# Output stores of two chunks on ScalarE's queue, and the first chunk's skip term added by VectorE: a change to a tuned state-space and feed-forward kernel

## The chip, the core and the metric

The kernel runs on one core of a Trainium2 chip. The metric is the device time of one execution in microseconds (us); several executions of each kernel were taken, and medians are quoted. An execution counts as fast or slow by its time and by the clock that TensorE was granted; ratios use the fast ones alone. The engines are TensorE (PE in the profile; PEld is its weight load), VectorE (DVE), ScalarE (ACT), GpSimd (POOL) and SyncE (SP), each with its own stream of instructions.

## The reference, cut to what matters

```
xn  = layernorm(x)                                    # x: 2048 tokens x 448, bf16
Bu  = xn @ B_bar.T                                    # complex
h_t = Lam_bar * h_{t-1} + Bu_t                        # recurrence over the tokens
s   = 2 * Re(h @ C.T) + xn * Dskip                    # the last product is the "skip"
g   = silu((silu(xn @ w_gate) * (xn @ w_up)) @ w_down)
out = x + s * g
```

The kernel takes the tokens in four chunks of 512, each of four blocks of 128 tokens.

## The kernel before: the parts that the change and the argument touch

The names in the profile: `gp`, `up` are the gate and up products, `gs`, `us` their values in SBUF, `Vt` their product, `hd` the down product, `sg` its silu; `pb` is the product with B, `ere`, `eim`, `bu_re`, `bu_im`, `H_re`, `H_im`, `tmp` belong to the recurrence; `y` is the product of the state with C; `t`, `ob` are the output's temporaries; `xT` is the normed input turned by DMA transposes that SyncE issues.

One chunk's output, and its skip term. In the kernel before, the first chunk's skip (and that of the last block) is made by TensorE with a diagonal matrix `Dd`; for the others VectorE multiplies and adds it:

```python
SKIPS = [(q, j) for q in (1, 2, 3) for j in range(TQ)][:-1]     # where VectorE adds the skip

def finish(q, j, y, sg, eng=nc.sync, c0=0, c1=D):
    ...
    if (q, j) in SKIPS:
        nc.vector.tensor_tensor(out=t[:], in0=y, in1=skip[q][:, j, c0:c1], op=ALU.add)
        y = t[:]
    nc.vector.tensor_tensor(out=t[:], in0=y, in1=sg[:, c0:c1], op=ALU.mult)
    ob = work.tile([P, c1 - c0], BF16, name="ob", **of)          # two buffers
    nc.vector.tensor_tensor(out=ob[:], in0=t[:], in1=x_all[:, m, c0:c1], op=ALU.add)
    eng.dma_start(out=out2d[m * P : (m + 1) * P, c0:c1], in_=ob[:])
```

The products that split K, the dimension that a matmul sums over, into two halves (`pb`, `gp`, `up`) run in two passes, and the second pass may start only after the first has finished. This notice travels by a no-op in GpSimd's stream:

```python
def tell(mm):
    told = nc.gpsimd.nop(nofuse=True)                            # waits for the matmul mm
    tc.add_manual_dep(told.ins, mm.ins.name, SYNC, reason="share")
    return told.ins.name

def sums(q, pairs, between=None):
    left = []
    for share, first in ((0, True), (1, False)):
        for n, two in enumerate(pairs):
            ...                                                  # the matmuls
                    if not first and m == 0:
                        told_of(mm, left[n])                     # second pass waits for the no-op
            if first:
                left.append(tell(mm))
```

The norms of the third and fourth chunk: ScalarE sums and squares (`junk`), GpSimd makes the root (three small operations), ScalarE then norms:

```python
def act_root(q):                                                 # on GpSimd
    nc.gpsimd.tensor_scalar(out=vep[...], in0=sums_of[:, 1, :], ...)
    nc.gpsimd.tensor_tensor(out=rstd[...], in0=vep[...], in1=halves[:], op=ALU.pow)
    nc.gpsimd.tensor_tensor(out=off_of[:, 1, :], in0=off_of[:, 0, :], in1=rstd[...], op=ALU.mult)
```

The order of the middle of the program:

```python
turned_norms(8, 9, 10, 11)           # ScalarE norms of the third chunk, SyncE's transposes
outs(0, sg)                          # output of the first chunk
sg = downs(1, 2.4, {
    0: act_sums((12, 13, 14), 0) + [on(skips, 2)],
    1: act_sums((15,), 0) + [act_means] + act_sums((12, 13), 1),
    2: act_sums((14, 15), 1) + [on(act_root, 3)],                # roots of the fourth chunk
})
drive(2, 4.8)                        # pb of the third chunk
gu(2, bg, 2.4)                       # gate and up of the third chunk
```

## Time and profile before

| | |
|---|---|
| time | 187.42 us (median of 4, 186.88 to 187.54) |
| span of the profiled execution | 185.0 us |
| busy: TensorE, VectorE, ScalarE, GpSimd | 177.9, 160.1, 120.2, 13.4 us |
| TensorE's one gap in the middle | 1.26 us, before `hd` of the third chunk |
| VectorE's one long gap | 7.7 us, before the first chunk's third `ob` |

What it does not show, and what decided the case, is GpSimd. Its timeline in the kernel before (columns: start, length, engine, line, operation, and in brackets the idle time and what ended it), in the middle of the program:

```profile
88.44 0.39 POOL L274 TENSOR_SCALAR vep<-sums_of 128x4 f32<-128x4 f32 x1 [11.50 <-ACT junk L263]
88.92 1.01 POOL L278 TENSOR_TENSOR rstd<-vep,halves 128x4 f32<-128x4 f32 x1
90.00 0.22 POOL L281 TENSOR_TENSOR off_of<-off_of,rstd 128x4 f32<-128x4 f32 x1
```

These are the fourth chunk's roots: GpSimd waits for ScalarE's last square, then works until 90.22. The second of them, the power operation, ends at 88.92 + 1.01 = 89.93. TensorE's timeline of the same time:

```profile
89.04 5.47 PE L455 MATMUL pb<-xT,BT 64*128 64x512 bf16 x56
```

The 56 `pb` matmuls of the third chunk run in one piece. The first passes of the first two products (16 matmuls) take 1.73 us at the pace of 0.216 us a pair, so TensorE needs the notice at 89.04 + 1.73 = 90.77. When could it have had it? In the five profiles below in which TensorE waits for these roots (the changed kernel, e5 to e8), it goes on 0.11 or 0.12 us after the power operation has ended; the third root operation, which still runs then, does not hold the notice. That makes 89.93 + 0.11 = 90.04 here. The reserve was thus about 0.7 us (an estimate from these times), and no row of the page shows it.

### The profile page before, as it was taken

Reading aid. Unit: us, or ns where it says so; the run is one execution under the profiler, and the core shown is the slowest. Engines: PE = TensorE matmul, PEld = TensorE weight load, DVE = VectorE, ACT = ScalarE, POOL = GpSimd, SP = SyncE. Lnnn points to the kernel's source line nnn. Section 1 sums busy time; section 2 is a strip of 40 time slices with the busy share of each in tenths; the row PEclk is TensorE's granted clock in tenths of the full one; section 3 lists DMA queues with packets and bytes.
Section 4 is the critical chain, followed back from the end, with each engine's and each line's share of the span. In section 5 each row is a group of like instructions: output and inputs, shape, how many; then the busy total and the mean of one; then the engine's idle time right before and its main releaser. Section 6 shows DMA issues by size and latency. Waiting matters only on the chain.

```text
span 185.0 us, 3723 instructions
## 1 busy us (share of the span) xinstructions
PE 177.9 (96%) x1449; PEld 87.8 (47%) x1449; DVE 160.1 (87%) x254; ACT 120.2 (65%) x247; POOL 13.4 (7%) x25
## 2 busy tenths in 40 slices
PE   7899999999999999999999999979999999999991
PEld 3574444544444555555454444535454444455551
DVE  4649799999999999902999999999999999999583
ACT  3247879997789999498499556962259696512110
POOL 7332200000000000600300000000000000000000
PEclk9999999999999999999999999999999999999999
DMA  5899655979200000043100000042100000001111
GB/s 160 209 277 338 124 94 112 132 167 377 101 0 0 5 0 0 0 86 81 50 2 4 2 0 4 0 82 70 62 4 0 0 4 0 0 4 50 50 50 50
DMA packets 26129, 12.71 MB, mean 69 GB/s; under 512 B 16000, under 2 KB 26112, under 8 KB 26112
## 3 DMA queue, kind: packets, MB, share of 16 engines
q1 hardware_dynamic: 24896, 12.06, 25.3%
q10 hardware_dynamic: 1088, 0.41, 0.8%
q8 instruction: 11, 0.18, 0.4%
q14 instruction: 6, 0.05, 0.1%
q0 software_dynamic: 128, 0.00, 0.0%
HBM read 7.23 MB, written 1.84 MB: 49 GB/s over the span
## 4 chain that ended last, share of the span: by engine, by line
PE 67%; DVE 25%; DMA 3%; issue 2%; ACT 1%; POOL 0%; SPq 0%; DVEq 0%
PE gp L455 20%; PE hd L597 16%; PE up L455 15%; PE pb L455 9%; PE y L626 7%; DVE bu_re L527 5%; DVE bu_im L527 4%; DVE tmp L521 2%; DVE Vt L589 2%; DVE ob L648 2%; DMA out_dram<-ob 2%; DVE t L645 2%; DVE H_im L521 2%; DVE ere L521 1%; DMA x_all<-in_A_x_dram 1%
## 5 line engine op out<-in xcount | busy, mean ns | idle before, releaser
L455 PE MATMUL gp<-xT,Wg 64*128 64x512 bf16 (+1 forms) x413 | 85.8, 365 | 0.4 <-ACT xT L304 0.3
L455 PE MATMUL up<-xT,Wu 64*128 64x512 bf16 (+1 forms) x413 | 85.8, 365 | 0.0
L455 PEld LDWEIGHTS <-Wg 64*128 64x128 bf16 x413 | 38.5, 94 | 25.1 <-issue 0.4
L455 PEld LDWEIGHTS <-Wu 64*128 64x128 bf16 x413 | 38.4, 94 | 19.7 <-POOLq L437 0.5
L581 ACT ACTIVATE gs<-gp 128x512 bf16<-128x512 f32 x56 | 33.7, 604 | 19.6 <-PE gp L455 11.7
L597 PE MATMUL hd<-Wd,Vt 128*128 128x448 bf16 x224 | 43.4, 353 | 1.3 <-DVE Vt L589 1.3
L585 ACT ACTIVATE us<-up 128x512 bf16<-128x512 f32 x54 | 32.9, 609 | 0.0
L597 PEld LDWEIGHTS <-Vt 128*128 128x128 bf16 x224 | 21.8, 98 | 22.0 <-DVE Vt L589 1.7
L602 ACT ACTIVATE sg<-hd 128x448 bf16<-128x448 f32 x16 | 8.6, 538 | 25.2 <-PE hd L597 20.6
L455 PE MATMUL pb<-xT,BT 64*128 64x512 bf16 (+1 forms) x224 | 21.9, 349 | 0.0
L648 DVE TENSOR_TENSOR ob<-t,x_all 128x448 bf16<-128x448 f32 (+2 forms) x17 | 10.2, 597 | 8.2 <-DMA out_dram<-ob 7.7
L589 DVE TENSOR_TENSOR Vt<-gs,us 128x2048 bf16<-128x2048 bf16 (+1 forms) x16 | 17.2, 1079 | 0.0
L455 PEld LDWEIGHTS <-BT 64*128 64x128 bf16 x224 | 10.7, 94 | 11.4 <-issue 0.7
L626 PE MATMUL y<-C,H_re 128*128 128x448 bf16 (+2 forms) x68 | 15.7, 342 | 0.0
L527 DVE TENSOR_TENSOR_SCAN bu_re<-rcol,H_re,ere 128x512 bf16<-128x512 f32 x12 | 14.9, 1262 | 0.1
L488 ACT ACTIVATE bu_re<-pb 128x512 bf16<-128x512 f32 (+1 forms) x20 | 10.1, 537 | 2.7 <-PE pb L455 2.6
L626 PE MATMUL y<-C,H_im 128*128 128x448 bf16 (+2 forms) x51 | 11.9, 342 | 0.0
L498 ACT ACTIVATE bu_im<-bu_re 64x512 bf16<-64x512 bf16 x16 | 10.0, 628 | 2.1 <-DVE bu_re L527 1.8
L527 DVE TENSOR_TENSOR_SCAN bu_im<-rcol,H_im,eim 128x512 bf16<-128x512 f32 x9 | 11.4, 1262 | 0.0
L287 ACT ACTIVATE xn<-x_all,off_of,rstd 128x384 bf16<-128x384 bf16 (+1 forms) x16 | 8.1, 588 | 2.8 <-POOL off_of L281 2.8
L521 DVE TENSOR_TENSOR tmp<-bu_im,ST 128x2048 bf16<-128x2048 bf16 x8 | 9.7, 1218 | 0.0
L626 PEld LDWEIGHTS <-H_re 128*128 128x128 bf16 x68 | 6.4, 98 | 6.1 <-issue 0.4
(98 smaller groups left out, 174.5 us busy)
## 6 DMA issues: line engine op xcount, KB each, us to landing
out_dram<-ob SPq DMA_DIRECT2D x15, 112.0 KB, 1.7
Wd<-in_B_w_down_dram SPq DMA_DIRECT2D x1, 1568.0 KB, 9.0
x_all<-in_A_x_dram SPq DMA_DIRECT2D x1, 896.0 KB, 5.5
Wg<-in_B_w_gate_dram SPq DMA_DIRECT2D x2, 384.0 KB, 7.0
Wu<-in_B_w_up_dram SPq DMA_DIRECT2D x2, 384.0 KB, 7.6
x_all<-in_A_x_dram SPq DMA_DIRECT2D x1, 448.0 KB, 5.7
Wg<-in_B_w_gate_dram SPq DMA_DIRECT2D x1, 288.0 KB, 3.1
Wu<-in_B_w_up_dram SPq DMA_DIRECT2D x1, 288.0 KB, 4.2
```

What stands on the lines that cost most here:

```text
L455: mm = nc.tensor.matmul(out, lhsT=w[h, d, :], rhs=xT[h, d, q * W + c0 : q * W + c1], start=(first and m == 0), stop=(not first and m == 3 ...
L488: nc.scalar.activation(to, pair[i][0], ACT.Copy)
L498: nc.scalar.activation(out[a], in_[b], ACT.Copy)
L521: nc.vector.tensor_tensor(out=of(out, n), in0=of(a, n), in1=of(b, n), op=op)
L527: nc.vector.tensor_tensor_scan(out=T["b"][c][:, k, :], data0=rcol[:, k : k + 1].to_broadcast([P, W]), data1=T["e"][c][:, k, :], initial=in ...
L581: nc.scalar.activation(gs[:, i + j, :], gp_[:], ACT.Silu)
L585: nc.scalar.activation(us[:, i + j, :], up_[:], ACT.Copy)
L589: nc.vector.tensor_tensor(out=Vt[:, f0 : f0 + n, :], in0=gs[:, 0:n, :], in1=us[:, 0:n, :], op=ALU.mult)
L597: nc.tensor.matmul(hd, lhsT=Vt_of[q][:, fi, j * P : (j + 1) * P], rhs=Wd[:, fi, :], start=(fi == 0), stop=(fi == NF - 1),)
L602: nc.scalar.activation(sg[:], hd, ACT.Silu)
L626: nc.tensor.matmul(y[:, c0:c1], lhsT=h, rhs=C2[:, n, c0:c1], start=(n == 0), stop=(n == NS - 1))
L648: nc.vector.tensor_tensor(out=ob[:], in0=t[:], in1=x_all[:, m, c0:c1], op=ALU.add)
```

## The change

Its intent: stores that sit on SyncE behind the transposes hold VectorE for 7.7 us, so ScalarE issues the stores of the first two chunks; and TensorE is the bound, so the first chunk's skip matmuls go to VectorE. The first chunk's norms have been overwritten by then, so ScalarE makes them again, into the tile that takes the skip. The smaller number in `downs` is the VectorE work that is slipped in between the blocks; with it, steps of the recurrence move behind the output. Cut to its core:

```diff
-    SKIPS = [(q, j) for q in (1, 2, 3) for j in range(TQ)][:-1]
+    SKIPS = [(q, j) for q in range(NQ) for j in range(TQ)][:-1]
...
+    def first_norms():
+        for j in range(TQ):
+            nc.scalar.activation(
+                skip[0][:, j, :], x_all[:, j, :], ACT.Identity, bias=off_0[:, j : j + 1],
+                scale=rstd[:, j : j + 1],
+            )
...
-    def outs(q, sg, hooks={}):
+    def outs(q, sg, eng=nc.sync):
         for j in range(len(sg)):
-            finish(q, j, out_sum(q, j), sg[j])
+            finish(q, j, out_sum(q, j), sg[j], eng)
...
-    sg = downs(0, 1.8, {
+    sg = downs(0, 1.3, {
...
-        2: act_sums((10, 11), 1) + [on(act_root, 2), on(skips, 1)],
+        2: act_sums((10, 11), 1) + [on(act_root, 2), on(skip_tile, 0), on(skip_tile, 1),
+                                    first_norms, on(skips, 1)],
+        3: [on(skips, 0)],
     })
...
-    outs(0, sg)
+    outs(0, sg, nc.scalar)
...
-    outs(1, sg)
+    outs(1, sg, nc.scalar)
```

More of the change, by code (lines that the diff above doesn't have):

```diff
@@ L258 @@
     off_of = ctile([P, 2, TQ], F32, "off_of")
+    off_0 = ctile([P, TQ], F32, "off_0")
     def act_sum(n, squares):
@@ L605, with skip_tile @@
     skip = {}
-    SKIPS = [(q, j) for q in (1, 2, 3) for j in range(TQ)][:-1]
+    SKIPS = [(q, j) for q in range(NQ) for j in range(TQ)][:-1]
+    def skip_tile(q):
+        skip[q] = work.tile([P, TQ, D], BF16, name="skip", tag="nz")
     def skips(q):
-        skip[q] = work.tile([P, TQ, D], BF16, name="skip", tag="nz")
         for j in range(TQ):
-            for c0, c1, x0 in ((0, KF * P, 0), (KF * P, D, KF * P + R)):
+            parts = [(0, KF * P, 0), (KF * P, D, KF * P + R)] if q else [(0, D, 0)]
+            for c0, c1, x0 in parts:
+                normed = xn[j][:, x0 : x0 + c1 - c0] if q else skip[q][:, j, :]
                 nc.vector.tensor_tensor(
-                    out=skip[q][:, j, c0:c1], in0=xn[j][:, x0 : x0 + c1 - c0],
-                    in1=skip["row"][:, c0:c1], op=ALU.mult,
-                )
+                    out=skip[q][:, j, c0:c1], in0=normed, in1=skip["row"][:, c0:c1], op=ALU.mult
+                )
+    def first_norms():
[4 more added lines that the diff above has]
+            )
     def out_sum(q, j, k0=0, k1=KT):
@@ L721, in drive @@
             params_out()
+            nc.vector.scalar_tensor_tensor(
+                out=off_0[:], in0=mv[:, 0:TQ, 0], scalar=-1.0, in1=rstd[:, 0:TQ],
+                op0=ALU.mult, op1=ALU.mult,
+            )
         ssm_steps(bg, q)
@@ L732, in downs @@
         return sg
-    def outs(q, sg, hooks={}):
+    def outs(q, sg, eng=nc.sync):
         for j in range(len(sg)):
-            finish(q, j, out_sum(q, j), sg[j])
-            for fn in hooks.get(j, ()):
-                fn()
-    def do(fns):
-        for fn in fns:
-            fn()
+            finish(q, j, out_sum(q, j), sg[j], eng)
     gu(0, bg, 0.0, {
@@ L772 @@
     turned_norms(8, 9, 10, 11)
-    outs(0, sg)
+    outs(0, sg, nc.scalar)
     sg = downs(1, 2.4, {
-        0: act_sums((12, 13, 14), 0) + [on(skips, 2)],
+        0: act_sums((12, 13, 14), 0) + [on(skip_tile, 2), on(skips, 2)],
         1: act_sums((15,), 0) + [act_means] + act_sums((12, 13), 1),
@@ L782 @@
     turned_norms(12, 13, 14, 15)
-    outs(1, sg)
-    sg = downs(2, 2.4, {1: [on(skips, 3)]})
+    outs(1, sg, nc.scalar)
+    sg = downs(2, 2.4, {1: [on(skip_tile, 3), on(skips, 3)]})
     drive(3, 4.8)
```

## The prediction

> **What bounds the kernel now.** I read the page's busy row first, then the chain of waits, the list of who waited for whom, and the timeline of each engine from 57 us on.
>
> The page, part 1, and two groups of its part 5:
>
> ```profile
> PE 177.9 (96%) x1449; PEld 87.8 (47%) x1449; DVE 160.1 (87%) x254; ACT 120.2 (65%) x247; POOL 13.4 (7%) x25
> ...
> L597 PE MATMUL hd<-Wd,Vt 128*128 128x448 bf16 x224 | 43.4, 353 | 1.3 <-DVE Vt L589 1.3
> ...
> L648 DVE TENSOR_TENSOR ob<-t,x_all 128x448 bf16<-128x448 f32 (+2 forms) x17 | 10.2, 597 | 8.2 <-DMA out_dram<-ob 7.7
> ```
>
> TensorE is busy for 177.9 of 185.0 us. Its starts show it streaming at a steady pace (a pair of K=64 matmuls every 0.216 us, a 448-column one every 0.19 us), so this is real work. In the timeline its only gap between about 19 and 181 us is one of 1.26 us, before `hd` of the third chunk, where it waits for the last `Vt` of that chunk. VectorE's one long gap is 7.7 us, for a store to land. The chain of waits ties the two together:
>
> ```profile
> 81.74 0.61 ACT junk L263 x3
> 82.36 0.31 issue
> 82.86 0.36 SPq L309
> 83.32 3.33 DMA out_dram<-ob
> 86.74 0.64 DVE ob L648
> ...
> 120.64 1.12 DVE Vt L589
> 121.75 1.21 DVE bu_im L527
> 122.98 0.96 DVE H_im L521
> 123.94 0.61 DVE Vt L589
> 124.60 8.50 PE hd L597 x44
> ```
>
> (Start, length, work.) The stores of the first chunk sit on SyncE behind four transposes whose inputs ScalarE makes from 76.98 to 81.02 us. The first store is issued at 83.32 and lands at 86.65. `ob` has two buffers, so the third `ob` waits. VectorE then works without a gap until 123.94+0.61, where TensorE has lost 1.26 us. From 124.6 us TensorE streams again until about 181; after that comes the tail of the last chunk, which the change leaves alone. So 7.7 us of VectorE waiting cost only 1.26 us of time.
>
> **What the Trainium skill says.** "PSUM — Partial Sum Buffer", Engine vs sequencer instructions: "ScalarE/VectorE/GpSimdE queues are strict FIFO." That decides this case: a store put into ScalarE's stream waits there for its `ob`, and all of ScalarE's later work waits with it. The trace shows the like on SyncE (stores behind transposes). "DMA: Bandwidth & Descriptors", Issuing engines are not separate DMA queues: transfers of different issuers run on the same 16 DMA engines and interleave, and only issue time is saved. So a store issued by ScalarE among the transposes need not land faster; here stores took 1.7 us in the median, and 3.3 us right behind the transposes. "VectorE: DVE Perf Modes", The perf-mode tier table: tensor_tensor runs at 2x on bf16 in SBUF and at 1x with an fp32 or PSUM operand. The trace agrees: 0.62 us for 128x448 with `y` from PSUM, against 0.35 us for the 128x384 bf16 `skip`.
>
> **The change part by part.**
>
> 1. TensorE: 16 skip matmuls of the first chunk go. Its four `y` start at 72.27, 73.79, 75.31 and 76.83, 1.52 us apart; those of the second chunk, without skip matmuls, start 1.33 us apart (115.59, 116.93). Saved: 4 x 0.19 = 0.75 us, on TensorE's path. All other TensorE work keeps its order.
>
> 2. VectorE: four skip products of 128x448 (an estimate from 0.37 us for a 384+64 pair: about 0.3 each, 1.2 in all), four additions at 0.66 us of spacing (2.6), and one tiny operation (0.2, like its neighbours at 36 to 38 us). Added: 4.0 us.
>
> 3. ScalarE: four norms of 128x448 at about 0.6 us (as the squares and the `c_tb` of this size) = 2.4 us. They come after the last squares (73.68 us) and before `sg` of the fourth block, in the hole of 2.77 us in which ScalarE waits for GpSimd's roots (73.68+0.53 to 76.98). So they are nearly free to ScalarE: 73.68+2.4+0.5 = 76.6, and the next norms still begin at 76.98 and end at 81.02.
>
> 4. Order: the smaller budget puts two steps (`tmp`, `ere`: 1.14+1.24) of the second chunk's recurrence behind its output instead of before it, and a scan and an `H_im` step (1.2+0.9 = 2.1 us) of the third chunk behind its last `Vt`. The comparison of the instruction orders shows this.
>
> VectorE in the new order: `H_re` done at 65.1 (+0.2); four `C` paced by `c_tb`, to 68.4; `eim`, to 69.2; eight skip products, 70.7; `tmp` and `eim`, 72.6. Then it must wait for the new norms, made at 74.3 to 76.1. That is a new wait of about 2.8 us in all: skip products done at 76.5, `ere` at 77.7. Four outputs at 2.05 us (the pace of 124.46, 126.50, 128.55): `ob` at 79.7, 81.8, then the third. ScalarE can issue the first store only after its norms, at 81.05, and it lands between 82.8 and 84.4 (1.7 to 3.3 us); the third `ob` would start at 83.1, so it waits 0 to 1.3 us. Outputs done at 86 to 87.2. Third chunk's skips 1.5, `tmp` and `ere` 2.4: the scans start at 89.9 to 91.1, where they started at 90.2. Of the 7.7 us, then, 4 go to new work, 2.8 to a new wait, and up to 1.3 stay: nearly nothing is left. The last `Vt` of the third chunk profits by the order alone: 2.1 us earlier, so at about 122.2 to 123.4 instead of 124.55.
>
> ScalarE: the fourth store is issued at 86.4 to 87.6; call it S. Only then can it turn to `sg` of the second chunk's first block, done before at 81.2. From there to the last of these `sg` it needs the work of 81.2 to 88.36 without its gaps, plus one `sg`: about 7.0 us. So the last `sg` ends at S+7.0 = 93.4 to 94.6, and before at 89.7.
>
> TensorE: `hd` of the second chunk would end 0.75 us earlier, at 88.4; the first `pb` group takes until 91.1 (2.65), and 0.86 later its second group turns to the packed pair, which takes the PSUM banks of the last two `hd` (eight banks in rotation: four `hd`, four `pb`, then these). They are free only after that last `sg`. So TensorE stops at 92.0 and goes on at 93.5 to 94.7: a new wait of 1.5 to 2.7 us. The gate and up matmuls of the third chunk then start at 95.0 to 96.2 instead of 94.35, that is 0.65 to 1.85 later. The 1.26 us lost before `hd` goes in exchange, since `Vt` is now there first. Net for the rest of the program: -0.6 to +0.6 us. TensorE's path in one sum: -0.75 (skip matmuls) -1.26 (wait for `Vt`) +2.1 (wait for the bank, the middle) = +0.1.
>
> The second set of stores on ScalarE costs nothing: before, `sg` of the third chunk waited for VectorE anyway (2.40 us for `t`, at 125.83), since `sg` has four buffers. By the same steps its fourth store comes near 131.5 and the last `sg` near 134.5, before the packed `pb` pair at about 136. VectorE's total up to the last chunk is unchanged within 1 us, and it had 1.9 us to spare there (its wait for `y` at 174.36).
>
> **The rivals.**
>
> A, the intended one: ScalarE gets through in time, and both small gains come to TensorE: 0.75+1.26 = 2.0 us, so 185.4 us. For it: TensorE has no other gap, and the packed `pb` pair was reached about 3 us after its `sg` in the trace (92.7 against 89.7). Against it: the fourth store holds ScalarE some 5 us longer than that.
>
> B, the one that I take: a wait for a PSUM bank behind ScalarE replaces the wait for `Vt`. The sum gives 187.5; if the stores land quickly and ScalarE's work packs tighter, 186.6.
>
> C, VectorE stays the bound: if the first store lands late and the new norms are slower, the scans start over 1.5 us later, the `Vt` come later in the third and fourth chunk, and ScalarE is held longer: 188 to 188.5. For it: VectorE has next to no reserve from 86 to 172 us, and gets 4.0 us more work. Against it: 2.1 us have moved behind the critical `Vt`.
>
> **Range and chances.** The three ways lie between 185.4 and 188.5. I give B the greatest weight and move the point a little towards A, since S rests on the landing of one store and on estimates for the norms, both taken on the slow side: 187.0 us, 185.7 to 188.1 eight times in ten. A gain over 2% (3.7 us) would need more than TensorE's gap and the removed matmuls together, and nothing else before 181 us is idle: 1 in 50. A loss over 2% would need a stall of ScalarE that holds up TensorE for over 5.7 us: 1 in 50. Within 2%: 0.96.
>
> **What would show it.** The steps are right if the profile of the changed kernel has: no wait of 7.7 us before `ob`, but one before the `skip` products for ScalarE's norms, near 73 us; ScalarE without work for about 5 us after 81 us and `sg` of the second chunk not before 86 us; a gap of TensorE before `pb`, released by ScalarE's `sg`, near 92 us; and no gap before `hd` near 124 us. The prediction is wrong if TensorE has no gap at `pb` (then A), if it still waits for `Vt` near 124 us (then C), or if stores and norms on ScalarE open a gap in the gate and up matmuls, which I put at none.

## More of the kernel before

One row of part 5 of the page does show that TensorE waits on GpSimd's sequencer at all (POOLq, at the line of the no-op), earlier in the program:

```profile
L455 PEld LDWEIGHTS <-Wu 64*128 64x128 bf16 x413 | 38.4, 94 | 19.7 <-POOLq L437 0.5
```

## The result, and the profile after

The changed kernel took 193.19 us (median of 4, 192.67 to 193.74), the kernel before 187.42. The ratio is 1.031 (95% interval 1.028 to 1.035): slower. Ratios here are the mean time of one kernel's fast runs over that of the other's in the same rounds, so not quite the ratio of the medians. The predicted 187.0 is 6.2 us too low, and the upper end of its range (185.7 to 188.1) 5.1 us.

The page of the changed kernel, parts 1, 2 and 5 (the clock row is the granted TensorE clock in tenths, in 40 slices of the span):

```profile
PE 179.2 (94%) x1433; PEld 87.8 (46%) x1433; DVE 164.3 (86%) x263; ACT 122.5 (64%) x251; POOL 13.0 (7%) x25
...
PEclk9999999999999999999969999999999999999999
...
L598 PE MATMUL hd<-Wd,Vt 128*128 128x448 bf16 x224 | 43.2, 352 | 0.0
...
L456 PE MATMUL pb<-xT,BT 64*128 64x512 bf16 (+1 forms) x224 | 23.6, 366 | 5.5 <-POOLq L438 5.5
...
L660 DVE TENSOR_TENSOR ob<-t,x_all 128x448 bf16<-128x448 f32 (+2 forms) x17 | 10.2, 598 | 1.1 <-DMA out_dram<-ob 0.6
```

Both waits that the change aimed at are gone: `hd` waits 0.0 us, and `ob` 0.6 us for a store where it was 7.7. In their place, `pb` waits 5.5 us for the line of the no-op in GpSimd's sequencer. And one slice has a clock of 0.6. The chain of waits shows how it came to that (start, length, work; the short pieces named "issue" are left out):

```profile
85.43 0.64 DVE ob L660
86.08 0.34 ACTq L661
86.47 0.54 ACT sg L603
87.01 1.67 ACT junk L264 x6
88.68 0.43 ACT sg L603
89.11 0.56 ACT junk L264 x2
89.70 0.21 ACT off_of L271
89.94 1.41 ACT junk L264 x4
91.35 0.43 ACT sg L603
91.78 1.31 ACT junk L264 x4
93.17 0.43 POOL vep L275
93.67 1.91 POOL rstd L279
95.62 0.03 POOLq L438
95.69 5.29 PE pb L456 x40
100.99 0.21 PE gp L456
```

Read it from the top. VectorE ends the fourth `ob`; ScalarE issues its store at 86.08 and only then turns to `sg` and to the squares (`junk`) of the fourth chunk, the last of which ends near 93.1. GpSimd's roots need these squares. The notice for `pb` stands behind the roots in GpSimd's stream: the no-op (POOLq) runs at 95.62, 0.04 us after the power operation has ended, and TensorE goes on at 95.69. (The third root operation runs from 95.66 to 95.95 and is not in the chain.) TensorE's timeline beside it:

```profile
88.29 1.90 PE L456 MATMUL pb<-xT,BT 64*128 64x512 bf16 x16
95.69 5.29 PE L456 MATMUL pb<-xT,BT 64*128 64x512 bf16 x40 [5.50 <-POOLq L438]
```

It stops after the 16 matmuls of the first pass. The following 40 then take 5.29 us. In runs shown further down, the same 40 take 3.74 us. The stretch view (columns: window, its length, busy time of TensorE, weight loads, VectorE, ScalarE and GpSimd with counts, granted clock, DMA share, GB/s) tells why:

```profile
95.70:98.40 2.70, 2.70 (x14) 1.04 (x16) 2.67 (x4) 1.08 (x2) 0.25 (x1) 0.50 0.00 0
98.40:101.00 2.60, 2.60 (x32) 1.40 (x28) 2.56 (x3) 1.38 (x3) 0.00 (x0) 0.91 0.00 0
```

After the stop, TensorE ran at half clock. Stretches of 0.2 us put the fall near 95.45, 5.3 us after TensorE stopped, and the return near 98.87: about 3.4 us, of which 3.2 had work. So the stop cost 5.50 us of waiting and 5.29 - 3.74 = 1.55 us of slow work.

VectorE's timeline of the changed kernel, for the prediction's steps:

```profile
74.50 0.39 DVE L618 TENSOR_TENSOR skip<-skip,skip_row 128x448 bf16<-128x448 bf16 x1 [1.76 <-ACT skip L625]
...
89.97 2.46 DVE L528 TENSOR_TENSOR_SCAN bu_re<-rcol,H_re,ere 128x512 bf16<-128x512 f32 x2
...
104.95 1.23 DVE L522 TENSOR_TENSOR tmp<-bu_im,ST 128x2048 bf16<-128x2048 bf16 x1 [2.65 <-ACT bu_im L499]
```

The new wait for ScalarE's norms is there at 74.5, and the scans start at 89.97. The wait at 104.95 is a consequence of the stop: ScalarE's copies of `pb` came late.

### The profile page after: what moved, and what is told of

It reads as the page before. It is cut to its first block, busy times and chain, and to the rows that moved or that the text cites. A ratio compares the mean times of both kernels' runs of the same rounds, so it can differ in the third digit from the quotient of the medians.

```text
span 190.5 us, 3700 instructions
## 1 busy us (share of the span) xinstructions
PE 179.2 (94%) x1433; PEld 87.8 (46%) x1433; DVE 164.3 (86%) x263; ACT 122.5 (64%) x251; POOL 13.0 (7%) x25
## 4 chain that ended last, share of the span: by engine, by line
PE 77%; ACT 9%; DVE 9%; issue 2%; POOL 1%; ACTq 0%; DVEq 0%; POOLq 0%
PE gp L456 25%; PE up L456 19%; PE hd L598 11%; PE pb L456 11%; PE y L638 6%; ACT junk L264 5%; DVE ob L660 3%; DVE t L657 3%; PE warm L179 2%; DVE t L655 2%; ACT skip L625 1%; ACT c_tb L420 1%; ACT sg L603 1%; POOL rstd L279 1%; PE tp L299 1%
## 5 line engine op out<-in xcount | busy, mean ns | idle before, releaser
L456 PE MATMUL pb<-xT,BT 64*128 64x512 bf16 (+1 forms) x224 | 23.6, 366 | 5.5 <-POOLq L438 5.5
L638 PE MATMUL y<-C,H_re 128*128 128x448 bf16 (+2 forms) x68 | 15.1, 342 | 0.0
L655 DVE TENSOR_TENSOR t<-y,skip 128x448 f32<-128x448 f32 x15 | 9.3, 623 | 2.7 <-PE y L638 1.5
L657 DVE TENSOR_TENSOR t<-t,sg 128x448 f32<-128x448 f32 x15 | 9.4, 625 | 0.8
```

The source lines that it names most:

```text
L456: mm = nc.tensor.matmul(out, lhsT=w[h, d, :], rhs=xT[h, d, q * W + c0 : q * W + c1], start=(first and m == 0), stop=(not first and m == 3 ...
L638: nc.tensor.matmul(y[:, c0:c1], lhsT=h, rhs=C2[:, n, c0:c1], start=(n == 0), stop=(n == NS - 1))
```

## The experiments

Theory G: the cause is a chain through GpSimd's stream. The fourth store holds ScalarE, so the fourth chunk's squares are late; GpSimd's roots wait for them; the notice stands behind the roots; TensorE waits for the notice and loses its clock. Rival B, the prediction's own: ScalarE's late `sg` holds the PSUM banks, and that is all. A second rival: the added work of VectorE and ScalarE is what costs. Eleven runs were made. All gave correct results.

### e1: the roots behind the notice

```diff
-        2: act_sums((14, 15), 1) + [on(act_root, 3)],
+        2: act_sums((14, 15), 1),
     })
     drive(2, 4.8)
+    act_root(3)
```

> The changed kernel with one edit: GpSimd's three small root operations for the fourth chunk stand behind the third chunk's pb matmuls in its stream, not ahead of them. Theory G (GpSimd's stream: the notice that lets pb's second half start stands behind those roots, and they behind ScalarE's late squares): the gap of 5.5 us before pb goes; what is left is the wait for ScalarE's last sg of the second chunk (about 93.5 us), a gap of 1.5 to 2 us near 92 us; no gap before hd; time 186.5 to 187.5, ratio to before 0.995 to 1.0. Rival B (PSUM banks and ScalarE's blocking are the whole cause, the notice only shows it): the gap stays at 4 us or more and the time within 1 us of 193.2.

Measured: 187.04 us (before, in the same rounds: 186.86), ratio 1.0009 (0.9991 to 1.0027). TensorE's timeline:

```profile
88.18 4.16 PE L456 MATMUL pb<-xT,BT 64*128 64x512 bf16 x37
93.44 1.57 PE L456 MATMUL pb<-xT,BT 64*128 64x256 bf16 x19 [1.09 <-ACT sg L603]
```

The 5.5 us wait is gone from an order of three small GpSimd operations. What is left is just the gap that the prediction had foreseen: at the packed pair (64x256), released by `sg`, 1.09 us. So Rival B's wait exists, but in the changed kernel it was hidden behind a longer one.

### e2: the notice by another engine

```diff
     def tell(mm):
-        told = nc.gpsimd.nop(nofuse=True)
+        told = relay["eng"].nop(nofuse=True)
...
+    relay["eng"] = nc.sync
     drive(2, 4.8)
+    relay["eng"] = nc.gpsimd
```

> The changed kernel with one edit: for the third chunk's pb matmuls alone, the notice between the two halves of TensorE's work is passed by SyncE, which is idle then, in place of GpSimd; the roots stay where they are. Theory G: as if the roots had been moved, 186.5 to 187.5 us, a gap of 1.5 to 2 us near 92 us. Rival B: no change, near 193 us. A second rival (the three root operations are slow in themselves, 2.5 us beside TensorE's work): near 193 us too, since they still run late, unless it is the notice alone that they hold.

Measured: 186.10 us, ratio 0.9963 (0.9948 to 0.9978), 0.4 us below the expected stretch. The roots ran as late as in the changed kernel (their power operation from 93.68 us), and cost nothing: TensorE had the same 1.10 us gap before the packed pair, released by `sg`. So neither the roots' work nor their lateness matters, only that the notice stood behind them. e1 and e2 agree on TensorE until the last chunk (its first `y` at 172.24 and 172.19 us, VectorE's end within 0.05 us); the 0.7 us between their profiled spans arose after VectorE's last instruction. Why it did, no run here tells.

### e3: the skip on VectorE alone, stores on SyncE

```diff
-    outs(0, sg, nc.scalar)
+    outs(0, sg)
...
-    outs(1, sg, nc.scalar)
+    outs(1, sg)
```

> The changed kernel with all stores back on SyncE: only the first chunk's skip moves to VectorE, with the reordering. Theory G: ScalarE isn't held (first sg of the second chunk near 81 us), no gap before pb; but VectorE's third ob waits for a store behind the transposes again (to about 86.5 us), so its scans start near 93 us and the last Vt of the third chunk is done near 125 us: a gap before hd of 2 to 2.6 us, time 187.5 to 188.5, ratio about 1.00 to 1.006. Rival (the added VectorE and ScalarE work is what costs 5.8 us): near 193 us.

Measured: 186.88 us, ratio 1.0002 (0.9978 to 1.0025). No gap before `pb`, and one of 1.28 us before `hd`, as in the kernel before. It was somewhat better than expected: the third `ob` started at 85.40, after a wait of 1.81 us, not at 86.5. The first store was issued no earlier than in the kernel before (83.41 against 83.32), but it landed after 1.90 us and not after 3.33; why, no run here tells. Four microseconds more of VectorE's work cost nothing in all. This rules out the second rival.

### e4 and e5: the stores on ScalarE alone

The kernel before, with

```diff
-    def outs(q, sg, hooks={}):
+    def outs(q, sg, hooks={}, eng=nc.sync):
         for j in range(len(sg)):
-            finish(q, j, out_sum(q, j), sg[j])
+            finish(q, j, out_sum(q, j), sg[j], eng)
...
-    outs(0, sg)
+    outs(0, sg, eng=nc.scalar)
...
-    outs(1, sg)
+    outs(1, sg, eng=nc.scalar)
```

> The kernel before with only its stores of the first two chunks moved to ScalarE. Theory G: VectorE's third ob no longer waits to 86.7 but to about 83.5 us, the fourth store leaves near 85 us, ScalarE's squares end near 91.5, the roots near 93 to 94.5, so a gap of 2.5 to 4 us before pb's second half from about 91 us, with a slow clock after it; time 189.5 to 191.5, ratio 1.01 to 1.022. Rival B (banks alone): the last sg at 92.4 is in time for the packed pair at 92.7, no gap, and the earlier Vt gives 186 to 187 us, ratio 0.993 to 0.998.

Measured: 186.07 us (the three fast executions alone: 185.92), ratio 0.9956 (0.9938 to 0.9973). My numbers missed. The profiled execution was no help: it took 322.86 us at a mean clock of 0.605, a slow execution, which the ratio leaves out. So the same kernel ran again:

> The same kernel as the run of the stores alone, whose profile fell into a slow clock (322.86 us), to see where its stall is. It ran in 186.07 us, against my 189.5 to 191.5. Theory G explains that if the two-operation outputs of VectorE let the fourth store go by about 83 us (GpSimd's roots at their short length, 1.0 us for the power, let ScalarE's norms begin near 75.7): then sg near 83.2, last squares near 89.9, roots done near 91.2 to 92.2, and the gap before pb's second half is 0.3 to 1.3 us, with none before hd. Rival B: no wait for a notice at all. Time 185.8 to 186.4 again.

Measured: 186.45 us (before: 187.08), ratio 0.9976 (0.9943 to 1.0008). The profile shows ScalarE's fourth store at 82.50 us, against 86.08 in the changed kernel, the last square done by 89.5, the power operation by 91.83, and before `pb`, at 91.94, the end of a wait of only 0.17 us, released by GpSimd's sequencer. (From 17.26 us on, TensorE's part of this execution stands 0.83 us later than in the kernel before, since it had waited 0.87 us for another notice there; GpSimd's power operation in front of that one began only at 17.22, where it began at 16.40.) My expectation for e4 had put VectorE's outputs too late: an output of two operations takes 1.43 us, not 2.05, and none had to wait long. So the chain is there, and with two VectorE operations an output it is just short enough. The reason that I gave beforehand for e5 was wrong in one point: the third chunk's power operation was long (1.99 us, as in the kernel before), not short, and ScalarE's norms began at 77.81.

So each half of the change is harmless alone (ratios 1.000 and 0.996 to 0.998), and the two together cost 3%: the skip makes the fourth `ob` later, and the store on ScalarE turns this into a late ScalarE.

### e6: ScalarE released one store earlier

```diff
-            finish(q, j, out_sum(q, j), sg[j], eng)
+            finish(q, j, out_sum(q, j), sg[j], eng if q or j < 3 else nc.sync)
```

> The changed kernel, but the first chunk's fourth store is issued by SyncE: ScalarE waits for the third ob (83.95 us), not for the fourth (86.05), so it is released 2.05 us earlier. Theory G: first sg of the second chunk near 84.4, last squares near 90.9, roots done at 92.2 to 93.6; the gap before pb's second half shrinks from 5.5 to 2 to 3.5 us; the slow clock after it shrinks or goes; time 187.5 to 189.5, ratio 1.003 to 1.014. Rival B: the last sg near 91.4 is just in time for the packed pair, no gap, 185.4.

Measured: 188.99 us (188.0 to 191.29), ratio 1.009 (1.0044 to 1.0136). The execution of 191.29 us counts as slow, and the ratio leaves it out; the median of the other three is 188.29. ScalarE's `sg` began at 84.40, and TensorE:

```profile
93.39 3.74 PE L456 MATMUL pb<-xT,BT 64*128 64x512 bf16 x40 [3.13 <-POOLq L438]
```

2.07 us less for ScalarE gave 5.50 - 3.13 = 2.37 us less of a gap. Releasing ScalarE earlier shortens the gap by about as much; of the extra 0.3 us, 0.23 come from GpSimd's first operation (0.19 us here, 0.42 there), and TensorE reached `pb` 0.07 us later. In this execution the clock stayed at full speed, and the 40 matmuls took 3.74 us. The mean clock of the others was 1.0 (188.0 us), 0.988 (189.69) and 0.979 (191.29).

### e7 and e8: two stores by ScalarE, two by SyncE

e7 has `j < 2` in place of `j < 3`; e8 also puts the second chunk's stores back on SyncE.

> The changed kernel, but of the first chunk's four stores the first two are issued by ScalarE and the last two by SyncE, which has sent its transposes off by then. ScalarE waits for the second ob only (81.9), sg near 82.4, last squares near 88.8, roots done at 90 to 91.5, as the notice is needed near 90.1: a gap of 0 to 1.4 us before pb; VectorE's third ob doesn't wait; no gap before hd. Theory G: 185.2 to 186.4 us, ratio 0.989 to 0.995, faster than the kernel before.

> As the run before it (two stores by ScalarE, two by SyncE), with the second chunk's stores back on SyncE. My claim that the second chunk's stores cost nothing where they stand: within 0.3 us of the run before it. Rival (ScalarE blocked near 128 to 133 us costs something too): over 0.5 us faster than the run before it.

Measured: e7 188.52 us, ratio 1.0064 (1.0024 to 1.0104); e8 187.10 us, ratio 1.0048 (0.9998 to 1.0097). Both missed: I had expected a win. ScalarE did go on at 82.1 to 82.4, and its last square ended at 88.7 and 89.0, 0.3 and 0.6 us later than in the kernel before. But GpSimd took longer over the roots. Its timeline in e7:

```profile
88.76 0.95 POOL L275 TENSOR_SCALAR vep<-sums_of 128x4 f32<-128x4 f32 x1 [13.42 <-ACT junk L264]
89.79 1.98 POOL L279 TENSOR_TENSOR rstd<-vep,halves 128x4 f32<-128x4 f32 x1
91.85 0.29 POOL L282 TENSOR_TENSOR off_of<-off_of,rstd 128x4 f32<-128x4 f32 x1
```

3.0 us from the start to the end of the power operation, against 1.5 in the kernel before. TensorE needed the notice at 88.03 + 1.73 = 89.76 and got it at 91.89, 2.1 us late: 1.5 from the longer roots, 0.3 from the squares, 1.0 since TensorE itself came 1.0 us earlier than before (89.04), less the reserve of 0.7. So the time that the change saves on TensorE eats the reserve as well. TensorE's timeline, first of e7:

```profile
91.89 5.42 PE L456 MATMUL pb<-xT,BT 64*128 64x512 bf16 x40 [1.96 <-POOLq L438]
```

and of e8:

```profile
92.18 3.74 PE L456 MATMUL pb<-xT,BT 64*128 64x512 bf16 x40 [1.96 <-POOLq L438]
```

The same wait of 1.96 us, and then 5.42 us for the work in one and 3.74 in the other. The granted clock between 94 and 96 us was 0.50 in e7's profile and 1.00 in e8's. In e7 it fell near 92.84, 0.95 us after TensorE had gone on, and was full again near 96.25. The executions of both kernels fall into two groups by their mean clock: e7 at 0.986 to 0.991 took 188.47 to 188.95 us and at 0.997 to 1.0 took 186.89 and 187.20; e8 at 0.988 and 0.991 took 189.21 and 189.09, at 0.996 to 1.0 186.83 to 187.10. So a wait of 2 us costs either 2 us or some 3.7; what decides which, no run here shows. That also spoils the comparison of e7 and e8 by medians (1.4 us apart, mostly from how many executions lost the clock). Within the groups their means differ by less than 0.1 us at full clock (two and four executions), and e8 is 0.4 us slower at the low one. So there is no sign that the second chunk's stores cost anything, though on few executions.

### e9 and e10: both cures together

e9 is e7 with the edit of e1; e10 is e7 with the edit of e2.

> The changed kernel with both cures: two of the first chunk's stores by ScalarE and two by SyncE, and the roots of the fourth chunk behind the third chunk's pb in GpSimd's stream. Theory G: no gap before pb (the last sg, near 88.9 us, is in time for the packed pair at 91.8, and the notice waits for nothing), none before hd; the saved skip matmuls and the lost wait before hd come through: 2.0 us less than the kernel before, ratio 0.987 to 0.991. No slow clock in any execution, so a narrow spread. If something else held TensorE near 92 us, a gap of over 0.3 us would stay.

> As the run before it, but the notice passes by SyncE for the third chunk's pb and the roots keep their place. Theory G: the same time within 0.3 us, ratio 0.987 to 0.991. If the roots themselves disturbed TensorE or VectorE there, the two would differ.

Measured, against 186.84 us for the kernel before: e9 185.32 us, ratio 0.9917 (0.9892 to 0.9941); e10 184.86 us, ratio 0.9897 (0.9872 to 0.9922). Both beat both kernels, though by less than the 2% that counts as a clear difference; e9's ratio lies just outside the expected 0.987 to 0.991, and the two differ by 0.46 us, not within 0.3. The spread is 0.8 us and 0.5 us, and all executions had a clock of 0.995 or more. TensorE's timeline in e10:

```profile
88.03 5.47 PE L458 MATMUL pb<-xT,BT 64*128 64x512 bf16 x56
```

One piece again, and `hd` of the third chunk waits for nothing. e9 is 0.5 us behind e10; its profile has a wait of 0.19 us for the notice at 95.67 us, where the roots now stand before the first notice of the gate and up products, and it entered `pb` 0.26 us later. The rest lies within the spread of the runs.

### e11: nothing but a later GpSimd

The kernel before, with three idle operations behind the roots:

```diff
-        2: act_sums((14, 15), 1) + [on(act_root, 3)],
+        2: act_sums((14, 15), 1) + [on(act_root, 3), on(busy_pool, 3)],
...
+    def busy_pool(n):
+        for _ in range(n):
+            nc.gpsimd.tensor_tensor(out=idle_p[:], in0=vep[:, 0:TQ], in1=halves[:], op=ALU.pow)
```

> The kernel before, with nothing but three more idle power operations on GpSimd (of 1.0 to 2.0 us each as the profile showed them) behind the roots of the fourth chunk, ahead of the notice. ScalarE, stores and skips are as they were. Theory G: GpSimd is free near 93.3 to 96 us where TensorE needs the notice near 90.9: a gap of 2.4 to 5 us before pb's second half, in part with a slow clock after it, less the 1.26 us before hd that it covers: 188.5 to 193 us, ratio 1.007 to 1.03. Rival (GpSimd's stream doesn't matter): 187 us, no gap before pb.

Measured: 187.41 us, ratio 1.0025 (0.9997 to 1.0053). GpSimd's timeline and, in a second fence, TensorE's:

```profile
90.51 3.53 POOL L289 TENSOR_TENSOR idle_p<-vep,halves 128x4 f32<-128x4 f32 x3
```

```profile
92.98 3.74 PE L461 MATMUL pb<-xT,BT 64*128 64x512 bf16 x40 [2.00 <-POOLq L443]
```

The gap came at the place that Theory G says, with ScalarE, stores and skips untouched. It was smaller than I had expected, since the three operations took 1.1 to 1.2 us each, near their short length, and since only two of them held the notice: TensorE went on 0.11 us after the second had ended (92.87), while the third ran until 94.04. The cost is smaller still: 2.00 us of a new wait less the 1.26 us before `hd`, which it covers, is 0.74 us; the medians differ by 0.57, and the interval of the ratio includes 1. So this run shows that the wait arises, not what it costs; the time missed the expected 188.5 to 193.

## Why the prediction was wrong

**What held.** The skip matmuls saved 0.75 us: `pb` began at 88.29 instead of 89.04. The four norms fitted into ScalarE's hole; VectorE waited for them (1.76 us, then three times 0.26), as foreseen. The scans started at 89.97 (foreseen 89.9 to 91.1). The fourth store left at 86.08, slightly before the foreseen 86.4 to 87.6; `sg` began at 86.47 and the last `sg` ended at 93.5 (foreseen 93.4 to 94.6). The wait before `hd` went. The PSUM wait at the packed pair exists, as e1 shows with 1.09 us; foreseen were 1.5 to 2.7. One small step was wrong without harm: the first store did not have to stay behind ScalarE's norms (foreseen at 81.05). It was issued at 79.87, as soon as its `ob` was done (79.84), while the last norm began only at 80.30, and so the third `ob` waited for nothing.

**What failed.** It is the step "TensorE: `hd` of the second chunk would end 0.75 us earlier ...", which went from the first `pb` group straight on to the PSUM banks and took `sg` to be the only thing that late ScalarE work holds up. It left out a second path from ScalarE to TensorE: squares, roots, notice. On that path the wait begins at the second pass of the first group and lasts until 95.69, beyond the end of the bank's wait. e1 and e2 each cut this path in another place, and both brought the time to 186 to 187 us, where the prediction had put it. e11 makes the wait without the change. So the sum's term "+2.1 (wait for the bank)" has to read +5.50 for the notice.

**The term that was not there.** After the stop TensorE worked at half clock: +1.55 us. All four executions of the changed kernel had a mean clock between 0.976 and 0.991. The Trainium skill's page "TensorE: Matmul & The Clock Gate" (Part 1: The HAM clock gate) describes a clock that halves after an idle window of about 3.4 us. This trace agrees: a stop of 5.50 us, and half clock from 5.3 us after its start. The prediction has no term for the clock; the gaps that it expected, 1.5 to 2.7 us, are shorter than that window.

The sum with measured terms: -0.75 + 5.50 + 1.55 - 1.26 = +5.0 us. TensorE reached the last chunk's first `y` at 178.03 instead of 173.00, which is +5.03. The profiled spans differ by 5.5 us, the medians by 5.8; the rest arises after that point and between executions (later ones had a lower mean clock than the profiled one), and isn't resolved further.

**The chances.** A loss over 2% got 1 in 50, on the ground that it would need a stall of over 5.7 us. The stall was there, at 5.5 us and its slow clock. The confidence rested on a list of TensorE's waits that left out a stream. Three readings would have found it: the row of the page with POOLq as releaser, the code of the no-op, and GpSimd's timeline beside TensorE's, where the end of the last root leaves 0.55 us, close to the 0.7 us that the later runs' 0.11 us gives.

**What the change was worth.** Its two ideas give 2.0 us (0.75 + 1.26), once nothing else holds TensorE: e10 is 1.98 us faster than the kernel before in the medians.

## What to carry to other kernels

When work is moved to an engine, or a wait is put into its stream, list everything that stands behind it there, and everything that waits for that work, no-ops that pass semaphores included; follow each such path to the engine that bounds the kernel, and work out its reserve. Two edits that are harmless alone can cost together when each uses up the same reserve. And a wait of TensorE is to be counted with the slow work that may follow it.

## What the Trainium skill lacked or had wrong

- "TensorE: Matmul & The Clock Gate", Part 1: The HAM clock gate, gives an idle window of about 3.4 us for the fall to half clock. Here a wait of only 1.96 us was followed by half clock in one execution (0.50 between 94 and 96 us, 40 matmuls in 5.42 us), and not in another (1.00, 3.74 us); four of six executions of e7 had the low mean clock. The page says that the window is free-running, and elsewhere that frequent short idles can make the clock swing; that a single idle time well below the window can cost the clock, it does not say.
- "SBUF — State Buffer", Who interferes with whom, says that a VectorE instruction with two SBUF inputs contends with a GpSimd instruction that reads SBUF, and that the second to issue blocks until the first is done. The traces agree with it but no run isolates it: the same 128x4 power operation took 1.01 us beside VectorE's short instructions (before, 88.92 us) and 1.98 us beside its scans (e7, 89.79 us), a difference of 0.97 us; the scan that ran when it began in e7 had about 1.1 us to go. The page gives no such figure for tiny GpSimd operations; here it was 0.97 of the 2.1 us by which the notice came late in e7.
- "PSUM — Partial Sum Buffer", Engine vs sequencer instructions, says that a no-op is run by the sequencer, which waits only until earlier instructions have been dispatched, not until they are complete. The traces agree: the no-op ran at 95.62 us, before the third root operation ended (95.95). The page warns that such a notice can come too early. That it can come too late, it does not say: here roots that waited for ScalarE stood in front of it, and TensorE stood still for 5.50 us.
